# The start of a fused attention and MoE kernel: first loads from two queues, held weights, copies in token order, zeroing on GpSimd

## The chip, the cores and the metric

One core of one Trainium2 chip. The time is device microseconds (us) of the core. Several runs of each kernel are taken, and a comparison uses runs of the same rounds on the same chip. All runs of this study are in the normal state ("fast"). They still differ in one thing, the clock that was granted to TensorE: the profile gives its mean for each run, and it lies between 0.976 and 1.000. The mean leaves something out: in the profiles the records of the clock begin only at 4.26 to 12.35 us, and what lies ahead of them is counted as whole.

Engines: PE is TensorE, PEld its weight loads, DVE is VectorE, ACT ScalarE, POOL GpSimd, SP SyncE. L412 is line 412 of a kernel; the same product has slightly different line numbers in each kernel.

## The reference, cut to what matters

```python
def _attn_ref(q, k, v, f_logit):              # (4, 8, 768, 48) each
    f = 1.0 / (1.0 + np.exp(-f_logit))
    for t in range(S):
        state = f[:, :, t, :, None] * state + einsum('bhd,bhe->bhde', k[:, :, t], v[:, :, t])
        y[:, :, t] = einsum('bhd,bhde->bhe', q[:, :, t], state)

def _moe_ref(x, domain_probs, w1, w2):        # x: (3072, 384), w1: (4, 384, 1024), w2: (4, 1024, 384)
    p = domain_probs / (domain_probs.sum(-1, keepdims=True) + 1e-09)
    for e in range(E):
        h = np.maximum(x @ w1[e], 0.0)
        out += p[:, e:e + 1] * (h @ w2[e])
```

The attention's output is the x of the MoE (mixture of experts).

## The kernel before: the parts that the argument touches

The 768 tokens are worked in six chunks of 128. A planner in the program fixes the order of every engine's instructions ahead of time. In the first chunk, each row of a tile holds two tokens, so that a load moves longer pieces. The loads of that chunk, the pieces of the weights, and their order:

```python
def load(c, nm, b, n):                        # chunk c, tensor nm, batch b
    if (c, nm) == (0, "v"):
        ins[c, nm, b] = nc.gpsimd.dma_start(...)           # v from POOL's queue
        if b in v_gate:
            after(ins[c, nm, b], ins[v_gate[b]])           # v of batch 0 waits for f of batch 1
        return
    if c == 0:
        ins[c, nm, b] = nc.sync.dma_start(...)             # f, k, q of chunk 0 from SP's queue
        return
    ins[c, nm, b] = nc.sync.dma_start(...)
    if (c, nm, b) == (1, "f", 0):
        after(ins[c, nm, b], ins["w", 6])                  # f of chunk 1 waits for the seventh piece of weights
    ...

def load_w(i, e, which, ks, cols):                         # piece i of the weights, from POOL's queue
    ins["w", i] = nc.gpsimd.dma_start(...)
    if i in w_hold:
        after(ins["w", i], ins[w_hold[i]])                 # w_hold = {1: (0, "k", 3)}: held until that load landed

def dma_kc(n):                                             # keys times gates, put back in token order: kc
    k = tl("qk", 0, n)[:, 1].rearrange("(p b) h d -> b p (h d)", b=2)
    for b in range(2):
        nc.sync.dma_start(out=kc[n // 2][...], in_=k[b])

def pe_kv0(g):                                             # new state = kc times v, for two batches
    ...  nc.tensor.matmul(out=tl("KV", 0, 2 * g + b)[...], lhsT=flat(kc[g][tok, i // 2], ...), ...)
# ... cut ...
```

`kc` goes by DMA from SBUF to SBUF, on SP's queue, behind f of chunk 1. Two zeroed buffers (Sf, and Sb twice) are filled by DVE. Q and K of the first chunk are copied out of PSUM in an order that puts even tokens first.

## Time and profile before

| | before |
|---|---|
| time, median of 4 runs | 306.87 us (306.65 to 307.14) |
| span of the profiled run, granted clock | 304.6 us, 0.983 |
| first product of the MoE | 23.40 us |
| kc landed | 46.7 to 49.1 us |
| kc used first | 49.25 us |
| kc used for batches 2 and 3 | 54.34 us |

The prediction below reads most of this profile. First TensorE in order of time, of the kernel before. The columns are start (us), busy time, engine, line, operation, output <- inputs, shape, count; a wait stands at the end in brackets.

```profile
43.97 0.81 PE L479 MATMUL ps_m<-xT,w_sb 128*128 128x512 bf16 x3
...
49.25 0.51 PE L417 MATMUL ps_t<-v,kc 64*128 64x96 bf16 x16
...
54.34 0.51 PE L417 MATMUL ps_t<-v,kc 64*128 64x96 bf16 x16
```

L479 is the first product of the MoE. L417 uses kc. The kc of these batches landed at 46.7 to about 48.1: the slack was about 1.2 us, no more. Then DVE in order of time, of the kernel before:

```profile
3.12 0.17 DVE L168 CAST parb<-par 128x2 bf16<-128x2 f32 x1
3.20 0.42 DVE L171 TENSOR_SCALAR Ui<-U,par 128x64 bf16<-128x64 f32 x2
...
7.71 0.54 DVE L349 TENSOR_TENSOR qk<-k,e 128x384 bf16<-128x384 f32 x1
```

L349 at 7.71 is the first product of keys and gates.

### The profile page before, as it was taken

How to read it: one execution, taken by the hardware profiler on the slowest of the kernel's cores; microseconds unless marked ns; L12 is line 12 of the kernel's file. 1: busy time of each engine (PE TensorE's matmuls, PEld its weight loads, DVE VectorE, ACT ScalarE, POOL GpSimd, SP SyncE). 2: the span in 40 equal slices, each digit the busy share in tenths (PEclk: the TensorE clock that was granted, in tenths of full speed). 3: DMA queues.
4: the chain of work that ended last, by engine and by line, in shares of the span. 5: the costliest groups of instructions: out<-in, count | busy, mean ns of one | idle time of the engine just before them, and what ended most of it. 6: DMA issues, size and time to landing. Idle time of an engine off the chain costs nothing.

```text
span 304.6 us, 5812 instructions
## 1 busy us (share of the span) xinstructions
PE 294.1 (97%) x2265; PEld 176.4 (58%) x2265; DVE 137.4 (45%) x275; ACT 170.7 (56%) x316; POOL 104.4 (34%) x178
## 2 busy tenths in 40 slices
PE   5969999999999999999999999999999999999995
PEld 2636865556776777455556455555555555555553
DVE  8754614697574586216465151534351322201223
ACT  4733554756757466776556765445565544465430
POOL 5192003718378359303628726224320000000000
PEclk9975999999999999999999999999999999999999
DMA  6999999992899987999796943001432100100002
GB/s 171 198 158 187 208 195 222 209 188 59 164 181 199 180 176 145 228 214 192 160 213 107 219 93 48 17 12 34 114 74 50 26 0 26 68 12 2 0 0 104
DMA packets 128975, 36.96 MB, mean 121 GB/s; under 512 B 118812, under 2 KB 128156, under 8 KB 128948
## 3 DMA queue, kind: packets, MB, share of 16 engines
q1 hardware_dynamic: 119748, 29.88, 48.9%
q0 software_dynamic: 9200, 6.72, 15.2%
q8 instruction: 17, 0.28, 0.4%
q14 instruction: 10, 0.08, 0.1%
HBM read 31.51 MB, written 4.72 MB: 119 GB/s over the span
## 4 chain that ended last, share of the span: by engine, by line
PE 87%; DMA 5%; SPq 5%; DVE 2%; ACT 1%; issue 0%; DVEq 0%
PE ps_m L479 39%; PE ps_m L494 39%; DMA q<-in_q_dram 3%; SPq L259 2%; DMA f<-in_f_logit_dram 2%; PE ps_t L425 2%; SPq L261 1%; PE ps_t L445 1%; PE ps_t L441 1%; PE ps_t L311 1%; PE ps_t L451 1%; PE ps_t L362 1%; DVE qk L349 1%; SPq L377 1%; PE ps_t L470 0%
## 5 line engine op out<-in xcount | busy, mean ns | idle before, releaser
L479 PE MATMUL ps_m<-xT,w_sb 128*128 128x512 bf16 (+1 forms) x720 | 155.6, 340 | 0.2 <-DVE pn L296 0.2
L490 ACT ACTIVATE h<-ps_m 128x512 bf16<-128x512 f32 (+1 forms) x188 | 99.6, 532 | 98.4 <-PE ps_m L479 96.1
L494 PE MATMUL ps_m<-w_sb,h 128*128 128x384 bf16 (+1 forms) x776 | 153.5, 324 | 0.0
L494 PEld LDWEIGHTS <-h 128*128 128x128 bf16 x776 | 74.6, 98 | 57.2
L479 PEld LDWEIGHTS <-w_sb 128*128 128x128 bf16 x720 | 68.7, 99 | 42.4 <-issue 0.6
L501 DVE SCALAR_TENSOR_TENSOR o<-ps_m,pn,o 128x384 f32<-128x384 f32 (+1 forms) x73 | 44.7, 612 | 106.2 <-PE ps_m L494 98.8
L488 DVE TENSOR_SCALAR h<-ps_m 128x256 bf16<-128x256 f32 (+1 forms) x52 | 25.0, 490 | 23.6 <-PE ps_m L479 21.1
L465 POOL TENSOR_TENSOR Sf<-Sf,egs 48x192 f32<-48x192 f32 x40 | 20.1, 501 | 43.6 <-DVE Sf L458 41.6
L353 POOL TENSOR_TENSOR qk<-q,e 128x384 bf16<-128x384 f32 x18 | 21.4, 1193 | 25.4 <-ACT e L336 23.1
L336 ACT ACTIVATE e<-ps_t 128x384 f32<-128x384 f32 x48 | 26.5, 667 | 4.3 <-PE ps_t L311 2.3
L434 DVE TENSOR_TENSOR AT<-ps_t,mask 128x512 bf16<-128x512 f32 x40 | 24.9, 683 | 4.8 <-PE ps_t L425 4.8
L247 POOL CAST vb<-v 128x384 bf16<-128x384 f32 x16 | 7.9, 507 | 34.7 <-issue 15.9
L353 POOL TENSOR_TENSOR qk<-k,e 128x384 bf16<-128x384 f32 x18 | 17.9, 998 | 4.5 <-DMA k<-in_k_dram 3.1
L458 DVE TENSOR_TENSOR Sf<-Sf,ps_t 48x192 f32<-48x192 f32 x40 | 14.0, 349 | 10.7 <-PE ps_t L451 8.2
L503 ACT ACTIVATE o<-ps_m,pn 128x384 f32<-128x384 f32 x22 | 12.8, 580 | 4.2 <-PE ps_m L494 3.3
L466 POOL CAST sb<-Sf 48x192 bf16<-48x192 f32 x40 | 14.1, 353 | 2.6
L299 ACT ACTIVATE ex<-f 128x768 f32<-128x768 f32 (+1 forms) x14 | 10.5, 747 | 6.9 <-DMA f<-in_f_logit_dram 6.9
L270 POOL DMA_DIRECT2D w_sb<-in_moe_w_dram x11 | 9.0, 818 | 6.8 <-DMA k<-in_k_dram 6.6
L306 ACT ACTIVATE gp<-ex 128x768 bf16<-128x768 f32 (+1 forms) x14 | 10.5, 751 | 0.4
L811 PE MATMUL ps_m<-busy 128*128 128x512 bf16 x19 | 8.9, 561 | 1.5 <-DVE busy L145 1.5
L445 PE MATMUL ps_t<-vb,AT 128*128 128x48 bf16 x160 | 10.0, 185 | 0.0
L343 POOL DMA_DIRECT2D egs<-e x16 | 9.0, 562 | 2.9 <-ACT e L336 2.9
(81 smaller groups left out, 143.2 us busy)
## 6 DMA issues: line engine op xcount, KB each, us to landing
w_sb<-in_moe_w_dram POOLq DMA_DIRECT2D x5, 768.0 KB, 15.8
k<-in_k_dram SPq DMA_DIRECT2D x10, 384.0 KB, 4.4
q<-in_q_dram SPq DMA_DIRECT2D x10, 384.0 KB, 5.5
v<-in_v_dram SPq DMA_DIRECT2D x10, 384.0 KB, 5.7
out_dram<-o SPq DMA_DIRECT2D x19, 192.0 KB, 2.1
f<-in_f_logit_dram SPq DMA_DIRECT2D x9, 384.0 KB, 5.1
w_sb<-in_moe_w_dram POOLq DMA_DIRECT2D x6, 384.0 KB, 7.3
f<-in_f_logit_dram SPq DMA_DIRECT2D x6, 192.0 KB, 4.2
```

What stands on the lines that cost most here:

```text
L336: nc.scalar.activation(out=o, in_=i, func=AF.Exp, scale=1.0 if j else -1.0)
L353: engines[eng].tensor_tensor(out=tl("qk", c, b)[:, j, :, 0:D].rearrange("t (i r) d -> t i r d", r=2), in0=tl("qk"[j], c, b // 2)[:, hh(b), ...
L434: nc.vector.tensor_tensor(out=tl("AT", c, b)[:, r].rearrange("s i t -> s (i t)"), in0=tl("A", c, b, r).rearrange("s i t -> s (i t)"), in1= ...
L445: nc.tensor.matmul(out=y[:, h * D:(h + 1) * D], lhsT=AT[:, r, i, :], rhs=vb[:, h, :], start=(c == 0), stop=True, skip_group_check=True)
L458: nc.vector.tensor_tensor(out=Sf[rows, b], in0=Sf[rows, b], in1=KV[rows, :, r, :], op=ALU.add)
L465: nc.gpsimd.tensor_tensor(out=Sf[rows, b], in0=Sf[rows, b], in1=eg, op=ALU.mult)
L466: nc.gpsimd.tensor_copy(out=nb[rows, b, :, r * D:(r + 1) * D], in_=Sf[rows, b])
L479: nc.tensor.matmul(out=hp(c, e, fc, n0, n1, nf)[:, f], lhsT=w1_sb[:, e, kk, (fc + f) * 128:(fc + f + 1) * 128], rhs=tl("xT", c)[:, kk, n0: ...
L488: nc.vector.tensor_relu(out=dst, in_=src)
L490: nc.scalar.activation(out=dst, in_=src, func=AF.Relu)
L494: nc.tensor.matmul(out=tl("op", c, e, nt, part)[:, cols], lhsT=tl("h", c, e, half_of(c, nt * T))[:, fc, nt * T:(nt + 1) * T], rhs=w2_sb[:, ...
L501: nc.vector.scalar_tensor_tensor(out=o, in0=op, scalar=pe, in1=o, op0=ALU.mult, op1=ALU.add)
```

## The change

It tries to bring the start of the MoE forward. The first loads come from two queues at once; the pieces of weights wait until loads of the later batches are through; the zeroing leaves DVE; the copies of Q and K become plain, and the matmul reads with a stride instead. The planner's costs are adjusted, which reorders TensorE's program.

```diff
-    nc.scalar.preload_act_table_set("natural_log_exp_and_others")
...
-    nc.vector.memset(Sf, 0.0)
+    nc.gpsimd.memset(Sf, 0.0)
...
-        nc.vector.memset(t, 0.0)
+        nc.gpsimd.memset(t, 0.0)
...
-            ins[c, nm, b] = nc.sync.dma_start(out=t[b % 2], in_=srcs[nm, 0][b])
+            ins[c, nm, b] = (nc.scalar if b == 1 else nc.sync).dma_start(out=t[b % 2], in_=srcs[nm, 0][b])
...
-        if c == 0:
-            o, i = o.rearrange("m q i (b p) -> m (q i) b p", b=2), i.rearrange("m q i (p b) -> m (q i) b p", b=2)
         copy(eng, o, i)
...
-        Q = QK[:, 0].rearrange("m (j i) t -> m i j t", i=2)
+        Q = QK[:, 0].rearrange("m (j i) (p b) -> m i b j p", i=2, b=2)
...
-                                         lhsT=QK[rows, 1, 2 * j + i, tok], rhs=Q[rows, i, :, tok], start=True, stop=True)
+                                         lhsT=QK[rows, 1, 2 * j + i, b::2], rhs=Q[rows, i, b], start=True, stop=True)
...
-    v_gate, w_hold, issued = {0: (0, "f", 1)}, {1: (0, "k", 3)}, []
+    v_gate, w_hold, issued = {0: (0, "f", 1)}, {0: (0, "k", 2), 1: (0, "q", 2)}, []
...
+        elif b == 1:
+            iss = P.add(f"issue {nm}", {"ACT": 0.65}, lambda _, nm=nm: load(0, nm, 1, 1), ...)
+            ...
+            if nm == "f":
+                P.add("table", {"ACT": 1.3}, lambda _: nc.scalar.preload_act_table_set("natural_log_exp_and_others"), ...)
... (planner costs and lags: cut)
```

More of the change, by code (lines that the diff above doesn't have):

```diff
@@ L45, in ready @@
                 return None
-            t = max(t, d.end + (d.lag + self.LATENCY if d.engine != e else 0.0 if e == "PE" else 0.05))
+            t = max(t, d.end + (d.lag + self.LATENCY if d.engine != e else 0.0 if e == "PE" or o.name.startswith("gate2 0.") else 0.05))
         return t
@@ L67, in run @@
         free_at = {e: 0.0 for o in left for e in o.costs}
-        free_at.update({"DMA": 0.8, "DVE": 5.0, "POOL": 3.5, "ACT": 2.1, "PE": 2.0})
+        free_at.update({"DMA": 0.8, "DVE": 5.4, "POOL": 4.6, "ACT": 0.7, "PE": 2.0})
         freeing, done, now = [], [], 0.0
@@ L517, in add_load @@
     def add_load(c, nm, b, n, prio, deps=(), cost=None):
-        op = P.add(f"ld {nm}{c}.{b}", {"DMA": cost or (1.05 if c else 0.65) * n}, lambda e: load(c, nm, b, n), prio,
-                   deps=deps, takes=[(nm, c, b // 2)], lag=2.0 if c else 1.65)
+        op = P.add(f"ld {nm}{c}.{b}", {"DMA": cost or (1.05 if c else 0.7) * n}, lambda e: load(c, nm, b, n), prio,
+                   deps=deps, takes=[(nm, c, b // 2)], lag=2.0 if c else 1.6 if b < 2 else 2.3)
         for i in range(n):
@@ L529, in add_v @@
                             deps=issued[-1:] + ([ld[v_gate[b]]] if b in v_gate else []), lag=1.2))
-        ld[0, "v", b] = P.add(f"ld v0.{b}", {"DMA": 0.65}, lambda _: None, prio, deps=issued[-1:], lag=1.6)
+        ld[0, "v", b] = P.add(f"ld v0.{b}", {"DMA": 0.75}, lambda _: None, prio, deps=issued[-1:], lag=1.3)
     for i, x in enumerate("f0 f1 k0 k1 q0 q1 v0 v1 f2 f3 k2 k3 q2 q3".split()):
@@ L535 @@
             add_v(b, -1000 + i)
+        elif b == 1:
+            iss = P.add(f"issue {nm}", {"ACT": 0.65}, lambda _, nm=nm: load(0, nm, 1, 1), -1100 + i, takes=[(nm, 0, 0)], lag=-0.2)
+            ld[0, nm, 1] = P.add(f"ld {nm}0.1", {"DMA": 0.7}, lambda _: None, -1000 + i, deps=[iss], lag=1.6)
+            if nm == "f":
+                P.add("table", {"ACT": 1.3}, lambda _: nc.scalar.preload_act_table_set("natural_log_exp_and_others"), -1100 + i + 0.5)
         else:
@@ L579, in attention0 @@
             pt_ = lambda kind, *x: ("ps_t", kind, 0, n) + x
-            g2 = P.add(f"gates 0.{n}", {"ACT": 0.95}, lambda _, n=n: [gate1(0, n, 1), gate2(0, n, 1)], s(0) - 0.5,
-                       deps=[ld[0, "f", 2 * g], ld[0, "f", 2 * g + 1]], takes=[("ex", 0, n), ("gp", 0, g)], frees=[("f", 0, g), ("ex", 0, n)])
-            cs = P.add(f"cs 0.{n}", {"PE": 0.5}, on(pe_cs, 0, n), s(0), deps=[g2], takes=[pt_("cs")], lag=0.2, frees=[("gp", 0, g)])
+            g1 = P.add(f"gate1 0.{n}", {"ACT": 0.53}, on(gate1, 0, n, 1), s(0) - 0.5, deps=[ld[0, "f", 2 * g], ld[0, "f", 2 * g + 1]],
+                       takes=[("ex", 0, n)], frees=[("f", 0, g)])
+            g2 = P.add(f"gate2 0.{n}", {"ACT": 0.53}, on(gate2, 0, n, 1), s(0) - 0.6, deps=[g1], takes=[("gp", 0, g)], frees=[("ex", 0, n)])
+            cs = P.add(f"cs 0.{n}", {"PE": 0.6}, on(pe_cs, 0, n), s(0), deps=[g2], takes=[pt_("cs")], lag=0.05, frees=[("gp", 0, g)])
             ek = P.add(f"expk 0.{n}", {"ACT": 0.41}, on(exps, 0, n, (1,)), s(0) + 0.1, deps=[cs], takes=[("e", 0, n)], frees=[pt_("cs")])
             eq = P.add(f"expq 0.{n}", {"ACT": 0.55}, on(exps, 0, n, (0,)), s(0) + 0.2, deps=[cs], takes=[("e", 0, n)], frees=[pt_("cs")])
-            pe = {"DVE": 0.5} if n < 2 else {"DVE": 0.5, "POOL": 1.2}
+            pe = {"DVE": 0.55} if n < 2 else {"DVE": 0.55, "POOL": 1.2}
             km = P.add(f"k 0.{n}", pe, one(product, 0, n, 1), s(4) - 0.2, deps=[ek, ld[0, "k", 2 * g], ld[0, "k", 2 * g + 1]],
@@ L590, in attention0 @@
             kcd[n] = P.add(f"kc 0.{n}", {"DMA": 0.4}, on(dma_kc, n), -453 + n, deps=[km, wd[2, 1][0]], frees=[("qk", 0, n)], lag=2.0)
-            tk = P.add(f"tpk 0.{n}", {"PE": 0.22}, on(pe_tp, 0, n, 1), s(4), deps=[km], takes=[pt_("tp")], frees=[("qk", 0, n)], lag=0.2)
-            tq = P.add(f"tpq 0.{n}", {"PE": 0.22}, on(pe_tp, 0, n, 0), s(4) + 0.01, deps=[qm], takes=[pt_("tp")], frees=[("qk", 0, n)], lag=0.2)
-            et = [P.add(f"ev_tp{j} 0.{n}", {"DVE": 0.36, "ACT": 0.5}, one(ev_tp, 0, n, slice(j, j + 1)), s(4) + 0.1, deps=[tj],
+            tk = P.add(f"tpk 0.{n}", {"PE": 0.4}, on(pe_tp, 0, n, 1), s(4), deps=[km], takes=[pt_("tp")], frees=[("qk", 0, n)], lag=0.05)
+            tq = P.add(f"tpq 0.{n}", {"PE": 0.4}, on(pe_tp, 0, n, 0), s(4) + 0.01, deps=[qm], takes=[pt_("tp")], frees=[("qk", 0, n)], lag=0.05)
+            et = [P.add(f"ev_tp{j} 0.{n}", {"DVE": 0.37, "ACT": 0.55}, one(ev_tp, 0, n, slice(j, j + 1)), s(4) + 0.1, deps=[tj],
                         takes=[("QK", 0, n)], frees=[pt_("tp")]) for j, tj in ((1, tk), (0, tq))]
-            at = P.add(f"at 0.{n}", {"PE": 0.5}, on(pe_at0, n), s(7), deps=et, takes=[a_key(n, r) for r in range(2)], lag=0.2, frees=[("QK", 0, n)])
+            at = P.add(f"at 0.{n}", {"PE": 0.5}, on(pe_at0, n), s(7), deps=et, takes=[a_key(n, r) for r in range(2)], lag=0.05, frees=[("QK", 0, n)])
             eA = [P.add(f"ev_at{r} 0.{n}", {"DVE": 0.62}, on(ev_at, 0, n, r), s(7) + 0.1 + 0.1 * r, deps=[at],
@@ L599, in attention0 @@
             N.append(P.add(f"y 0.{n}", {"PE": 0.5}, on(pe_y0, n), s(11), deps=eA + [ld[0, "v", 2 * g], ld[0, "v", 2 * g + 1]] + N[-1:] * (n % 2),
-                           takes=ys, frees=[("AT", 0, n)], lag=0.2))
+                           takes=ys, frees=[("AT", 0, n)], lag=0.05))
             for b in range(2 * g, 2 * g + 2) if n % 2 else ():
@@ L605, in attention0 @@
                 xk = ("ps_t", "xp", 0, b, 0)
-                xt = P.add(f"xt 0.{b}", {"PE": 0.17}, on(pe_xt, 0, b, slice(0, KD)), s(13) + 0.01 * b, deps=[ey], takes=[xk], frees=[("yb", 0, b)], lag=0.2)
+                xt = P.add(f"xt 0.{b}", {"PE": 0.17}, on(pe_xt, 0, b, slice(0, KD)), s(13) + 0.01 * b, deps=[ey], takes=[xk], frees=[("yb", 0, b)], lag=0.05)
                 xdone[0, b] = [P.add(f"ev_xt 0.{b}", {"ACT": 0.45, "DVE": 0.4},
@@ L613, in attention0 @@
             kv = P.add(f"kv 0.{g}", {"PE": 0.36}, on(pe_kv0, g), s15, deps=[kcd[2 * g], kcd[2 * g + 1], xdone[0, B - 1][0]],
-                       takes=[("ps_t", "KV", 0, b) for b in bs], lag=0.2)
+                       takes=[("ps_t", "KV", 0, b) for b in bs], lag=0.05)
             for b in bs:
@@ L747 @@
     pl = P.add("ld p", {"DMA": 0.2}, lambda e: load_p(), -989.5, lag=3.0)
-    pj = P.add("p by j", {"POOL": 0.8, "DVE": 0.6}, lambda e: p_by_j(e), -1.5, deps=[pl] + xdone[0, 1], takes=[("v", 0, 0)])
+    pj = P.add("p by j", {"POOL": 0.8, "DVE": 0.6}, lambda e: p_by_j(e), -1.5, deps=[pl] + xdone[0, B - 1], takes=[("v", 0, 0)])
     pp = P.add("pp", {"PE": 0.6}, lambda e: pe_pp(), -1, deps=[pj], takes=[("ps_m", "pp")], lag=0.2, frees=[("v", 0, 0)])
```

## The prediction

> **What bounds the kernel now.** I read the page first, then the chain of work that ended last, then the order of time on TensorE around the start of the MoE (mixture of experts: L479 is its first product, L494 its second), then busy time by stretch, then who waited for whom.
>
> The page:
>
> ```profile
> PE 294.1 (97%) x2265; PEld 176.4 (58%) x2265; DVE 137.4 (45%) x275; ACT 170.7 (56%) x316; POOL 104.4 (34%) x178
> ...
> PEclk9975999999999999999999999999999999999999
> DMA  6999999992899987999796943001432100100002
> ```
>
> TensorE is busy 97% of 304.6 us, and the waits of PE from 22 us to the end are two of 0.2 us. So the MoE stage runs at TensorE's pace, and this change removes none of its matmuls: it can only start it earlier, or run its beginning at a better clock. The third and fourth slice (15 to 30 us) have a low clock, and the DMA engines are busy nearly to 68 us.
>
> The chain of waits, first 30 us:
>
> ```profile
> 9.18 8.75 DMA q<-in_q_dram
> ...
> 18.05 1.84 DVE qk L349 x2
> ...
> 19.94 1.03 PE ps_t L362 x8
> ```
>
> The last load of the first 128 tokens (q of batch 3) lands at 17.9; its products and transposes follow. TensorE in order of time:
>
> ```profile
> 17.49 0.40 PE L362 MATMUL ps_t<-ident,qk 128*128 128x128 bf16 x4 [2.27 <-POOL qk L349]
> ...
> 19.94 1.03 PE L362 MATMUL ps_t<-ident,qk 128*128 128x128 bf16 x8 [0.66 <-DVE qk L349]
> 20.77 0.85 PE L470 MATMUL ps_t<-ident,yb 128*128 128x128 bf16 x6
> ...
> 23.40 0.82 PE L479 MATMUL ps_m<-xT,w_sb 128*128 128x256 bf16 x3
> ```
>
> TensorE takes instructions in program order. The transposes of batches 2 and 3 (L362, waiting for late loads) stand ahead of the transposes L470 of the finished batches 0 and 1. So the MoE starts at 23.40, though the first two batches were through their masking on DVE at 16.0.
>
> By stretch (us, PE, PEld, DVE, ACT, POOL busy, granted clock, DMA share, GB/s):
>
> ```profile
> 12.35:19.17 6.82, 4.44 (x95) 2.77 (x93) 4.20 (x7) 3.60 (x11) 3.49 (x4) 1.00 1.17 180
> ...
> 23.40:29.41 6.01, 6.01 (x62) 3.90 (x58) 2.38 (x5) 1.92 (x5) 1.70 (x3) 0.50 1.25 187
> 29.41:36.50 7.09, 6.87 (x74) 6.00 (x69) 5.42 (x15) 4.55 (x12) 0.00 (x0) 1.00 1.21 207
> ```
>
> The first 6.0 us of the MoE run at clock 0.50, so about 3.0 us are lost there: at full clock the same work would have started at 26.4.
>
> **What the Trainium skill says.** "TensorE: Matmul & The Clock Gate", part 1: the clock is halved after a window of some 3.4 us with little activity and given back after a busy one. The trace agrees in kind: PE stood still 2.27 us before 17.49, and the clock is 0.50 from 19.2 to 29.4, three such windows. "DMA: Bandwidth & Descriptors", "Issuing engines are not separate DMA queues": a second issuing engine saves only the sequencer's time. Before, one issue takes 0.64 us on SP and the first six loads land 0.8 us apart (3.8 to 7.9), so there is little to save. "VectorE: DVE Perf Modes", "Zero memsets can be issued as uint32": the trace has the two bf16 zeroings on DVE as 112x768 uint32, 0.70 each; the program of the changed kernel has them on POOL as 112x1536, twice the elements.
>
> **The change part by part.**
>
> 1. Loads of batch 1 from ACT. f of batch 1 is issued at 0.74 with f of batch 0 instead of 1.58; k and q of batch 1 come after the 1.28 us table load, at about 2.7 and 3.3. The first gate began at 5.11, when f of batch 1 had landed (4.7) and was seen; now about 4.3. Saves 0.8 on this chain.
>
> 2. Zeroing on POOL. DVE was in memsets to 7.68 (0.70 + 1.51) and began the first product at 7.71. Now it is free at 5.5, so the product starts when exp of k is ready, about 6.9. POOL pays: three fills of 128 f32 take 0.49, some 1.0 to 1.1 ns per element, so 768 + 2 x 1536 elements take 3.9 (estimate). POOL is free near 6.4, and v of batch 0 is issued at 6.4 instead of 5.32. It is needed by L409, at 14.67 before and about 12.2 after: close, but with fewer loads ahead of it.
>
> 3. Copies in token order. The eight copies of Q and K of 512 columns cost 0.69 on DVE and 0.58 on ACT; the new order sends the first four to ACT, so the four products run on DVE without a break (6.9 to 9.1; the fourth ended at 11.65). Then copies to 10.8 (from ACT's 8.5, 4 x 0.58), first masking at 10.7, 4 x 0.64, ended 13.3 instead of 16.0: 2.7 saved. The stride-2 reads move to L394 on PE, 16 matmuls in 0.42; even doubled that is 0.4 per batch.
>
> 4. Weights held. The first weight piece (issued at 6.87, landed 14.4) shared the engines with k and q of batches 2 and 3. A piece alone takes 2.0 us (landings 26.6, 28.5, 30.5). It now waits for k of batch 2, so q of batch 3 lands near 13 instead of 17.9 (12 loads at 0.75, two v at 0.8, from 2.2 us, plus latency).
>
> 5. Order on TensorE. The program now puts the last product of attention and the transposes L470 of batches 0 and 1 ahead of the transposes of batch 3, and moves the transposes of the probabilities (1.3 us at half clock) later. Working on: yb copied at about 15.6, batch 2's transposes and copies 15 to 16.2, scores 16.9, first L479 near **17.5** instead of 23.4. PE is thinly used from 10 to 17 us, so I expect half clock again for 6 to 8 us of the MoE: 3 to 4 us lost, against 3.0 before. The lead in full-clock terms is then 26.4 - 21 = about **5 us**.
>
> 6. What is behind: the transfers. Weight pieces 2 to 4 landed at 20.8, 23.3, 26.6, because they were issued at 15.6, 17.4, 19.4 behind waits. Now they can be issued from about 13 in one go. If the DMA engines work without a break from 2.2: 12 loads 9.4, four v 3.3, p 0.2, four pieces 8.0, and then the 21.9 us from 26.6 to 48.4 as before: all pieces but the last landed at 45.0 instead of 48.4. So the stream gains **3.4 us**. In it stands a stage with no slack: the reordered keys kc, issued after the sixth piece of weights and landing together:
>
> ```profile
> SPq L261 <- DMA w_sb<-in_moe_w_dram: 24.3, 1, 24.3
> ...
> SPq L374 <- DMA f<-in_f_logit_dram: 6.4, 1, 6.4
> ```
>
> The first kc for batches 0 and 1 were issued at 35.05 to 37.4 and landed 11.3 to 11.6 later, 46.7 to about 48; TensorE used them (L417) at 49.25. In the new program L417 stands one unit of seven matmuls (1.3 us) earlier. TensorE with a lead of 5 would come there at 43; kc would be there at about 44.6. Then the lead is the stream's: 3.4, or a bit less. After that, slack is larger (f of the next tokens landed 50.0, used 54.9), the last weight piece (67.0, needed 68.5) moves with both, and the load of f at 84.56 (0.2 us waited for) hangs on work that moves with TensorE.
>
> The sum: 306.7 - 3.5 = **303.2**.
>
> **The rivals.** (a) TensorE sets the gain alone: the stream advances as far as the head, or kc has more slack; then 5 us, 301.7, and with a full clock from the start 8, 298.5. For it: the steady state has no waits; against it: kc had 1.2 us of slack at most. (b) The stream gains little: holding the weights leaves the DMA engines idle while POOL, in program order, waits for the issue (DMA share fell to 0.77 at 16 to 18 us from such a wait). Then the MoE starts early and waits for its second to fourth piece, and a stop of 2 to 3 us halves the clock again: 305 to 306. For it: POOL now waits for two loads, not one, with v of batches 2 and 3 behind the first. (c) Zeroing on POOL delays v of batches 0 and 1, L409 waits, the head gains 3 instead of 6: about 304.5, as the stream still sets the later part. (d) A new wait at the next tokens' loads gives all back: 306.5; little speaks for it.
>
> **Range and chances.** The two limits are 5 +- 2 (clock) and 3.4 +- 1 (stream), the smaller counts. Range 300.4 to 305.6. Over 2% needs 300.7 or less, which wants (a) with a good clock: 0.14. Slower by 2% has no mechanism of that size: 0.02.
>
> **What would show it.** First L479 at 17 to 18.5 (right), at 20 or later (steps 3 to 5 wrong). First gate near 4.3; masking ended near 13.3; q of batch 3 landed near 13; pieces of weights landed without gaps, the ninth at about 45. Clock 0.5 in the first 6 us of the MoE. A wait of PE of 1 to 2 us before L417, or before a weight load near 19 to 23 us. The forecast is wrong upward if the clock is whole from the first L479 and kc lands before 42; wrong downward if PE waits over 2 us in several places from 18 to 50.

## The result, and the profile after

| | before | after |
|---|---|---|
| time, median of 4 runs | 306.87 us (306.65 to 307.14) | 303.46 us (301.41 to 304.13) |
| ratio after / before | | 0.9877, 95% 0.9828 to 0.9926 |
| span and clock of the profiled run | 304.6 us, 0.983 | 301.4 us, 0.994 |

A ratio here is the mean time of one kernel's fast runs over that of the other's of the same rounds, so it is not quite the ratio of the medians. The kernel is 1.2% faster, within 2% and inside the predicted range. A second set of five runs, later, gave 302.15 (below).

From the page of the changed kernel (busy time by engine, then the clock and the DMA engines in 40 slices of 7.5 us, then the chain by engine):

```profile
PE 290.9 (97%) x2261; PEld 173.2 (57%) x2261; DVE 133.9 (44%) x265; ACT 172.5 (57%) x323; POOL 107.5 (36%) x181
...
PEclk9999997999999999999999999999999999999999
DMA  7999999964979979999699952101432100100002
...
PE 83%; DMA 10%; SPq 3%; DVE 1%; POOL 1%; ACT 1%; issue 0%
```

The low clock has gone from the third and fourth slice, and a new low stands in the seventh (45 to 53 us). The chain of work that ended last now holds DMA for 10% of the span. TensorE in order of time, of the changed kernel:

```profile
16.94 0.83 PE L476 MATMUL ps_m<-xT,w_sb 128*128 128x256 bf16 x6
...
42.93 0.21 PE L414 MATMUL ps_t<-v,kc 64*128 64x96 bf16 x1 [1.12 <-DMA kc<-qk]
43.52 0.34 PE L414 MATMUL ps_t<-v,kc 64*128 64x96 bf16 x7 [0.38 <-DMA kc<-qk]
...
44.55 0.34 PE L414 MATMUL ps_t<-v,kc 64*128 64x96 bf16 x7 [0.31 <-DMA kc<-qk]
...
46.40 1.49 PE L476 MATMUL ps_m<-xT,w_sb 128*128 128x512 bf16 x3
...
51.80 0.51 PE L414 MATMUL ps_t<-v,kc 64*128 64x96 bf16 x16
```

The MoE starts at 16.94 instead of 23.40, and its first 512-column product at 36.46 instead of 43.97: at that point the lead is 7.5 us. Then TensorE stands before L414, where kc is used. The 16 matmuls that ran in one go in the kernel before now trickle from 42.93 to 44.89, as the transfers land. At 46.40 the same products take 1.49 instead of 0.81: half clock. Who waited for whom, PE from 18 us to the end, total, times, longest:

```profile
PE ps_t L414 <- DMA kc<-qk: 2.0, 4, 1.1
```

And by stretch (PE, PEld, DVE, ACT, POOL busy, granted clock, DMA share, GB/s):

```profile
36.50:45.84 9.34, 7.37 (x51) 3.71 (x50) 2.05 (x5) 3.13 (x6) 0.44 (x1) 1.00 1.12 204
45.84:49.25 3.41, 3.41 (x11) 1.43 (x10) 0.59 (x2) 1.03 (x2) 2.92 (x8) 0.50 1.20 229
```

PE is busy 7.37 of 9.34 us in the first stretch, and the next 3.41 us run at clock 0.50, which costs half of it, 1.7 us. The account of the profiled runs therefore closes: the last product with kc ended 49.77 before and 44.89 after, 4.9 earlier; minus 1.7 for the half clock is 3.2, and the spans differ by 304.6 - 301.4 = 3.2.

### The profile page after: what moved, and what is told of

It is laid out like the page before. It is cut to its first block, busy times and chain, and to the rows that moved or that the text cites. A ratio compares the mean times of both kernels' runs of the same rounds, so it can differ in the third digit from the quotient of the medians.

```text
span 301.4 us, 5811 instructions
## 1 busy us (share of the span) xinstructions
PE 290.9 (97%) x2261; PEld 173.2 (57%) x2261; DVE 133.9 (44%) x265; ACT 172.5 (57%) x323; POOL 107.5 (36%) x181
## 3 DMA queue, kind: packets, MB, share of 16 engines
q1 hardware_dynamic: 118164, 29.29, 48.4%
## 4 chain that ended last, share of the span: by engine, by line
PE 83%; DMA 10%; SPq 3%; DVE 1%; POOL 1%; ACT 1%; issue 0%
PE ps_m L491 38%; PE ps_m L476 38%; DMA kc<-qk 4%; DMA w_sb<-in_moe_w_dram 3%; DMA f<-in_f_logit_dram 2%; PE ps_t L422 2%; DMA k<-in_k_dram 2%; SPq L260 2%; PE ps_t L442 1%; SPq L258 1%; PE ps_t L438 1%; PE ps_t L310 1%; PE ps_t L448 1%; POOL w_sb L269 0%; POOL v L252 0%; SPq L374 0%
## 5 line engine op out<-in xcount | busy, mean ns | idle before, releaser
L487 ACT ACTIVATE h<-ps_m 128x512 bf16<-128x512 f32 (+1 forms) x188 | 98.4, 527 | 98.2 <-PE ps_m L476 96.0
L498 DVE SCALAR_TENSOR_TENSOR o<-ps_m,pn,o 128x384 f32<-128x384 f32 (+1 forms) x73 | 44.6, 611 | 108.6 <-PE ps_m L491 100.7
L476 PEld LDWEIGHTS <-w_sb 128*128 128x128 bf16 x720 | 68.0, 98 | 42.6 <-issue 1.5
L485 DVE TENSOR_SCALAR h<-ps_m 128x256 bf16<-128x256 f32 (+1 forms) x52 | 26.1, 510 | 22.8 <-PE ps_m L476 20.2
L246 POOL CAST vb<-v 128x384 bf16<-128x384 f32 x17 | 8.7, 523 | 32.1 <-issue 14.7
L455 DVE TENSOR_TENSOR Sf<-Sf,ps_t 48x192 f32<-48x192 f32 x40 | 14.0, 351 | 13.2 <-PE ps_t L448 9.6
L244 ACT CAST yb<-ps_t 128x384 bf16<-128x384 f32 x17 | 8.1, 476 | 6.2 <-PE ps_t L442 6.2
```

What stands on the lines that cost most here:

```text
L455: nc.vector.tensor_tensor(out=Sf[rows, b], in0=Sf[rows, b], in1=KV[rows, :, r, :], op=ALU.add)
L476: nc.tensor.matmul(out=hp(c, e, fc, n0, n1, nf)[:, f], lhsT=w1_sb[:, e, kk, (fc + f) * 128:(fc + f + 1) * 128], rhs=tl("xT", c)[:, kk, n0: ...
L485: nc.vector.tensor_relu(out=dst, in_=src)
L487: nc.scalar.activation(out=dst, in_=src, func=AF.Relu)
L498: nc.vector.scalar_tensor_tensor(out=o, in0=op, scalar=pe, in1=o, op0=ALU.mult, op1=ALU.add)
```

## The experiments

Twelve kernels ran in three sets, each set on one chip beside the kernel before (medians 306.29, 307.64 and 306.04, 9 to 11 runs). First the whole picture. The columns come from each trace: the start of the MoE, the landing of the first and last kc transfer, the first and last use of kc for batches 0 and 1, and the start of its use for batches 2 and 3 (second use).

| kernel | median us | ratio to before | MoE starts | kc landed | kc first use | second use | span | span minus second use |
|---|---|---|---|---|---|---|---|---|
| before | 306.87 | 1 | 23.40 | 46.7 to 49.1 | 49.25 to 49.77 | 54.34 | 304.6 | 250.3 |
| changed | 303.46 | 0.9877 | 16.94 | 42.9 to 45.6 | 42.93 to 44.89 | 51.80 | 301.4 | 249.6 |
| changed, again | 302.15 | 0.9863 | 17.72 | 43.1 to 45.5 | 43.12 to 45.09 | 50.32 | 299.7 | 249.4 |
| kc ahead of f | 299.04 | 0.9764 | 17.51 | 36.4 to 41.6 | 41.72 to 42.23 | 47.46 | 297.3 | 249.8 |
| fillers in the stop | 301.66 | 0.9850 | 17.71 | 43.0 to 45.1 | 44.51 to 45.02 | 50.25 | 300.1 | 249.8 |
| one queue only | 305.97 | 0.9983 | 18.41 | 45.3 to 47.6 | 45.39 to 47.22 | 53.74 | 303.4 | 249.7 |
| weights not held | 301.14 | 0.9823 | 18.20 | 42.1 to 44.4 | 42.41 to 43.91 | 49.13 | 299.1 | 250.0 |
| not held, kc first | 301.55 | 0.9842 | 19.98 | 35.8 to 40.8 | 44.19 to 44.70 | 49.93 | 299.4 | 249.5 |
| before, kc first | 304.92 | 0.9948 | 23.83 | 40.3 to 45.9 | 47.54 to 48.06 | 52.63 | 302.8 | 250.2 |
| before, two queues | 304.22 | 0.9932 | 21.59 | 45.4 to 47.8 | 45.41 to 47.32 | 51.90 | 301.7 | 249.8 |

The last column says where to look: from the second use of kc on, all these kernels need 249.4 to 250.3 us (the four of the last experiments, which are not in the table, 249.3 to 250.5). What this change gains or loses in these profiles is decided in the first 54 us.

My theory: two things can hold TensorE at about 42 to 48 us, the start of the MoE (the "head") and the landing of kc (the "stream"), and the later one counts. The rivals: the head alone sets the gain; or what matters is the clock, and the wait for kc is only where it shows.

### kc ahead of f (label e1_kcfirst)

The transfers of kc are issued on SP before f of chunk 1 instead of behind it; TensorE's order is kept.

```diff
     def load(c, nm, b, n, now=False):
+        if (c, nm, b) == (1, "f", 0) and not now:
+            return
...
     def dma_kc(n):
-            nc.sync.dma_start(out=kc[...], in_=k[b])
+            d = nc.sync.dma_start(out=kc[...], in_=k[b])
+            if (n, b) == (0, 0):
+                after(d, ins["w", 6])
+        if n == B - 1:
+            load(1, "f", 0, 1, True)
```

> The changed kernel with the eight transfers of reordered keys (kc) issued ahead of the first load of f of the next tokens, after the same (seventh) piece of weights; the order on every compute engine is unchanged. Theory (the gain is capped by kc, and the wait for it also costs a stretch of half clock): kc lands by 36, TensorE does not stop before L414 (2.9 us before), the clock stays whole from 4.9 us on, span 301.4 - 2.9 - 1.7 = 296.8, time near 298.7 (over 2.5% faster than the kernel before). Rival (the next loads give it back: f then lands later and TensorE stops at the next tokens' cumulative sums, L310, instead): time 301 to 303.

Measured: 299.04 us (298.73 to 299.16), ratio 0.9764 (0.9739 to 0.9788), clock 0.998 or more in every run. TensorE in order of time:

```profile
41.72 0.51 PE L420 MATMUL ps_t<-v,kc 64*128 64x96 bf16 x16
...
47.46 0.51 PE L420 MATMUL ps_t<-v,kc 64*128 64x96 bf16 x16
```

The 16 matmuls run in one go again, at 41.72. From issue to landing, the transfers of kc took (minimum, median, maximum), first in the changed kernel, then here:

```profile
DMA to landing us min/median/max: 3.2/10.5/11.5
```

```profile
DMA to landing us min/median/max: 5.3/6.0/6.7
```

In the changed kernel those of batches 0 and 1 took 10.9 to 11.5, issued behind f; the 3.2 is the last of the eight, issued only when f had landed. Here those of batches 0 and 1 landed at 36.4 to 39.5, a little later than the 36 expected, but in time. The stop and the half clock are both gone, and the rival's new stop did not come (TensorE waited 0.7 us at its cumulative sums, 0.6 in the changed kernel), so the theory holds: the changed kernel had been giving back 1.1% of the time, over 3 us (ratio 0.9764 against 0.9877), at this one place.

### Fillers in the stop (label e2_warm)

Twelve matmuls that nobody needs stand ahead of the first use of kc, so that TensorE has work while it would wait.

```diff
     def pe_kv0(g):
+        for _ in range(12 if g == 0 else 0):
+            nc.tensor.matmul(out=tl("KV", 0, 0), lhsT=busy[:, 0:128], rhs=busy, start=True, stop=True)
```

> The changed kernel with 12 matmuls of ones (128x512, 0.22 us each) on TensorE just ahead of the first L414, so that it is busy while it waits for kc. Theory (waiting and half clock are two costs, the second follows from the first): L414 still ends its wait at about 44.6, but the clock stays whole, 1.7 us less: span 299.7, time near 301.6. Rival (the clock drop at 45.8 has nothing to do with the stop): the drop remains, time 303.5 or a little more.

Measured: 301.66 us (301.25 to 302.13), ratio 0.9850 (0.9824 to 0.9875), clock 0.998 to 1.000. TensorE in order of time:

```profile
41.82 2.75 PE L411 MATMUL ps_t<-busy 128*128 128x512 bf16 x12
44.51 0.51 PE L416 MATMUL ps_t<-v,kc 64*128 64x96 bf16 x16
```

The fillers take the place of the wait, and the use of kc ends at 45.02, as late as without them (44.89, and 45.09 in the second profile below). The stop costs the same; the half clock behind it is taken away, in all five runs. So the clock is a second cost that follows from the stop, and the rival "it is the clock" is wrong for the larger part: with a whole clock in both, 301.66 - 299.04 = 2.6 us on the same chip are the stop, but for 0.2 us by which the MoE started later here.

### The changed kernel again (label e12_after)

> The changed kernel itself once more, on the chip of this call, so that the others can be read against it and so that chips can be told from kernels. Expected 302.5 to 303.9, ratio 0.985 to 0.991, a stop of 2 to 3 us before the key-value products and one window of half clock behind it. If the first submission was a chance of its chip, the ratio is outside that.

Measured: 302.15 us (301.44 to 303.67), ratio 0.9863 (0.9815 to 0.9911). TensorE in order of time:

```profile
43.12 0.21 PE L414 MATMUL ps_t<-v,kc 64*128 64x96 bf16 x1 [1.13 <-DMA kc<-qk]
43.70 0.70 PE L414 MATMUL ps_t<-v,kc 64*128 64x96 bf16 x8 [0.36 <-DMA kc<-qk]
...
50.32 0.52 PE L414 MATMUL ps_t<-v,kc 64*128 64x96 bf16 x16
```

The stop is the same, but in this profile no half clock followed, and the second use is at 50.32 instead of 51.80. The time is a little under the expected 302.5 to 303.9, and the expected window of half clock did not come in this profile. That is instructive. The nine runs of the changed kernel in both sets fall in two groups: clock 0.999 or 1.000, 301.41, 301.44, 301.45 and 302.15 us; clock 0.993 or 0.994, 303.18, 303.19, 303.67, 303.74 and 304.13. Their means are 1.97 us apart, near the 1.7 that one window of half clock costs. One window of 3.41 us at half clock in 301 us gives just that mean, 1 - 1.7 / 301 = 0.994. The stop is in both profiles; the half clock is in one, and by the clocks in five of the nine runs (where in those runs it fell is seen only in the profiled one).

The traces show part of the reason. Within a profile the changes of the clock lie multiples of 3.41 us apart (19.17 and 29.41 in the kernel before, 45.84 and 49.25 in the changed one), so the time can be cut into steps of 3.41 us from them. In the first profile one step (42.42 to 45.84) held most of the stop: PE was busy for 2.06 us of it. Here the stop fell across two steps, with 2.60 and 2.24 us busy. Of the other profiles with over 1 us of waits for kc, e3_zlate (1.04 busy in the emptiest step) and e5_sp (1.49) had a half clock behind the stop; e4_zdve (2.01) and e7_perm (2.54) had none. The emptiest steps had it, but 2.01 without and 2.06 with half clock show that the busy time alone does not decide it.

The clock at the start differs too, and the mean does not show it. In this profile the records begin at 12.10:

```profile
8.03 1.01 PE L814 MATMUL ps_m<-busy 128*128 128x512 bf16 x2
...
12.74 0.60 PE L814 MATMUL ps_m<-busy 128*128 128x512 bf16 x2
```

In the first profile such a pair took 0.59 already at 7.26. That profile had a favourable start: its MoE began at 16.94, here at 17.72.

### One queue only (label e5_sp)

```diff
-            ins[c, nm, b] = (nc.scalar if b == 1 else nc.sync).dma_start(out=t[b % 2], in_=srcs[nm, 0][b])
+            ins[c, nm, b] = nc.sync.dma_start(out=t[b % 2], in_=srcs[nm, 0][b])
```

> The changed kernel with the loads of batch 1 issued from SP again (one part undone). Theory: f of batch 1 lands at 4.7 instead of 3.9 and the first gate starts at 5.1, but the first cumulative sum moves by 0.3 us only, as it waited for VectorE; SP is busy for three more issues of 0.65 us, so k of batch 2 lands 1 us later, and with it weights and kc: time 303.9 to 304.6. Rival (transfers set the pace, a second issuing engine is worth nothing): 303.5.

Measured: 305.97 us (305.21 to 307.52), ratio 0.9983 (0.9923 to 1.0043). The loss is larger than I expected: without the second queue nearly the whole gain is gone. A part of it is the clock, as no run of this kernel was free of a half clock (0.989 or 0.993). Among the runs at 0.992 to 0.994 this kernel took 305.21 to 305.97 us, the changed kernel 303.18 to 304.13, and the kernel before, on the chip of this kernel, 305.55 and 305.62. So at like clock the queue is worth about 2.0 us, or 0.7%, and that is still nearly the whole gain. What that queue does is seen by stretch, from 2.75 to 8.25 us. First the kernel with one queue:

```profile
2.75:5.50 2.75, 1.45 (x4) 0.26 (x2) 2.72 (x6) 0.51 (x1) 2.75 (x3) 1.00 1.02 258
5.50:8.25 2.75, 2.13 (x18) 1.65 (x19) 2.56 (x11) 2.45 (x8) 1.89 (x3) 1.00 0.99 250
```

Then the changed kernel, with two:

```profile
2.75:5.50 2.75, 1.45 (x4) 0.27 (x2) 2.72 (x6) 0.91 (x3) 2.75 (x3) 1.00 1.13 308
5.50:8.25 2.75, 1.86 (x19) 1.09 (x20) 2.60 (x12) 2.55 (x8) 1.88 (x3) 1.00 1.18 326
```

The last column is what the DMA engines moved: 258 and 250 GB/s with SP's queue alone for f, k and q, 308 and 326 with two (POOL's queue, for v, is there in both). SP issues one load of 192 KB every 0.68 us in this trace, which is at most 289 GB/s (196,608 bytes over 0.68 us). One queue fed the engines more slowly than they could move. Their busy share, the column ahead, is 1.02 and 0.99 with one queue, and so would pass for engines at their limit.

q of batches 2 and 3 is issued from 7.33 us on with two queues and from 8.85 with one, and q of batch 3 lands at 12.39 instead of 14.05; the first piece of weights, held for k of batch 2, is issued at 9.87 instead of 12.02; kc lands 2.0 to 2.4 us earlier.

### The kernel before with the second queue alone (label e11_act_alone)

f, k and q of batch 1 are issued from ACT's queue, with the table load between f and k; nothing else.

```diff
-    nc.scalar.preload_act_table_set("natural_log_exp_and_others")
...
-            t = tl(nm, c, b // 2)[:].rearrange(...)
-            ins[c, nm, b] = nc.sync.dma_start(out=t[b % 2], in_=srcs[nm, 0][b])
+            for x in "fkq" if (nm, b) == ("f", 1) else nm if b != 1 else "":
+                t = tl(x, c, b // 2)[:].rearrange(...)
+                ins[c, x, b] = (nc.scalar if b == 1 else nc.sync).dma_start(out=t[b % 2], in_=srcs[x, 0][b])
+                if (x, b) == ("f", 1):
+                    nc.scalar.preload_act_table_set("natural_log_exp_and_others")
```

> The kernel before with one part of the change alone: f, k and q of batch 1 issued from ACT's queue (table load after f). Theory (the second issuing queue takes three issues of 0.65 us off SP, so that the loads of batches 2 and 3 start nearly 2 us earlier; q of batch 3 lands near 16.3 instead of 17.9, the first product of the MoE is at 21.8 instead of 23.4, and the weights behind it are earlier by as much): 304.8 to 305.6, ratio 0.994 to 0.997. Rival (the prediction's first step: little to save in the issuing): 306.2 to 306.8, ratio above 0.998.

Measured: 304.22 us (303.49 to 306.32), ratio 0.9932 (0.9882 to 0.9981), a little better than expected; the rival (above 0.998) lies at the very edge of the interval. At like clock (0.992 to 0.994) this kernel took 303.49 to 304.36 us and the kernel before, on the same chip, 305.49 to 306.04, so the rival is out. The MoE starts at 21.59 (expected 21.8), q of batch 3 lands at 16.31 (expected 16.3). TensorE in order of time, one of the uses of kc:

```profile
45.96 0.34 PE L419 MATMUL ps_t<-v,kc 64*128 64x96 bf16 x7 [0.33 <-DMA kc<-qk]
```

This one part, alone, brings 1 - 0.9932 = 0.7% of the 1.4% that the changed kernel brings in the same set, and already here TensorE arrives at kc before it has landed (0.8 us of waits): in this profile the stream is the limit from there on.

### Weights not held (label e6_unhold)

The changed kernel with the holds of the kernel before: the first piece free, the second behind k of batch 3.

```diff
-        if i in w_hold:
+        if i == 1:
+            after(ins["w", i], ins[0, "k", 3])
+        elif i in w_hold and i > 1:
             after(ins["w", i], ins[w_hold[i]])
```

> The changed kernel with the first piece of weights not held and the second held by k of batch 3, as before (one part undone). Theory: the first piece lands near 13, q of batch 3 near 15 instead of 12.4, first L476 at 18 to 19 instead of 16.9; the seventh piece of weights and kc land at most 1 us later, because the engines move the same bytes without a break: TensorE stops for kc for less time, total 303.3 to 304.5. Rival (the head counts): as much as L476 is late, 304.5 to 305.5.

Measured: 301.14 us (300.88 to 302.63), ratio 0.9823 (0.9771 to 0.9875). I expected a small loss against the changed kernel, and it came out no slower, if anything 0.4 to 0.5% faster (the intervals overlap; among the runs with a whole clock it took 300.88 to 301.14 us, the changed kernel 301.41 to 302.15). The head was later, 18.20 instead of 16.94, as expected. But the first piece of weights was issued at 7.36 instead of 9.87, the seventh landed at 29.79 instead of 30.89, and kc with it:

```profile
42.41 0.58 PE L416 MATMUL ps_t<-v,kc 64*128 64x96 bf16 x8
43.29 0.62 PE L416 MATMUL ps_t<-v,kc 64*128 64x96 bf16 x8 [0.30 <-DMA kc<-qk]
```

Waits of 0.30 and 0.06 are left of the 2.0. Holding the weights is good for the head (both profiles had a whole clock from 4.9 us or earlier), and in the changed kernel a later head costs nothing. That holding is bad for the stream is not shown: with the holds the seventh piece landed at 30.89 and 30.42 in the two profiles of the changed kernel and at 30.19 to 31.10 in e1_kcfirst, e2_warm and e7_perm, and in the second profile without holds (next) at 30.44.

### Weights not held, kc ahead of f (label e10_kc_unhold)

Two edits: one was faster alone, the other no slower.

> The changed kernel with both of the edits that were faster alone: kc ahead of f, and the first weights not held for the late loads. Theory A (with the stop at the key-value products gone, TensorE is bound by the start of the MoE alone; not holding costs 1.2 us there, 18.2 against 16.9 to 17.5, and the earlier stream is worth nothing more): 299.3 to 300.2, not faster than kc ahead of f alone (299.0). Theory B (the stream still sets a part): 297.5 to 298.6. Both: no wait for kc, whole clock from before the first product of the MoE.

Measured: 301.55 us (301.20 to 302.10), ratio 0.9842 (0.9785 to 0.9898). Neither forecast was met: it is slower than kc ahead of f with the holds kept (299.04, ratio 0.9764), by more than theory A put. With kc out of the way the head counts, and the head suffers. Who waited for whom on PE from 16 us, then TensorE in order of time:

```profile
PE ps_t L365 <- DVE qk L352: 1.5, 1, 1.5
```

```profile
16.69 0.61 PE L365 MATMUL ps_t<-ident,qk 128*128 128x128 bf16 x4 [1.55 <-DVE qk L352]
...
19.98 0.83 PE L484 MATMUL ps_m<-xT,w_sb 128*128 128x256 bf16 x6
```

The transposes of batch 2 wait 1.55 us for their products, as they did in the kernel before, and a window of half clock (16.17 to 19.58) falls on the last steps ahead of the MoE: it starts at 19.98. That is 2.5 us later than with the holds, and the second use of kc is 2.5 later too (49.93 and 47.46). So the same edit costs nothing, or gains some 0.5%, where the stream is the limit, and loses about 0.8% where the head is. Not all of the 2.5 us need be the edit: in the profile above, with the same first loads and no holds, the clock was whole from 4.75 on and the MoE started at 18.20. Here it was whole from 9.34 on, as with kc ahead of f (9.37), but then fell, which it did not there. Three of the four runs had a clock of 0.994; the one at 1.000 took 301.28, so the loss does not hang on that window alone. (The two kernels with kc first ran on different chips; their ratios are each to the kernel before on the same chip.)

### The kernel before with kc ahead of f (label e9_bkc)

> Control: the kernel before, with kc issued ahead of f of the next tokens and right after the seventh piece of weights, the same edit that brought the changed kernel to 299.0. Theory (kc ahead of f only takes away TensorE's stop before the key-value products, which the kernel before doesn't have: its kc landed by 48 and was used at 49.25): the same as the kernel before within 0.5 us, ratio 0.998 to 1.002, first product of the MoE at 23.4, key-value products at 49.2. Rival (the order of kc and f is worth something by itself, apart from the stop): 303 to 305, ratio below 0.995.

Measured: 304.92 us (304.57 to 305.86), ratio 0.9948 (0.9905 to 0.9992). My forecast of no effect is missed by about 1 us, and the rival's numbers fit. I had reckoned with the one profile of the kernel before, in which kc had 1.2 us of slack and a half clock over the first 6 us of the MoE. In this profile the half clock fell at 12.55 to 22.79, ahead of the MoE at 23.83, and kc was used at 47.54, 1.7 earlier than in that profile, when the kernel before would not have had all of it.

```profile
47.54 0.52 PE L423 MATMUL ps_t<-v,kc 64*128 64x96 bf16 x16
```

A floor fits that: the profiled run of the kernel before took 306.4, and minus 1.2 of slack is 305.2; of its 29 runs in the three sets the lowest is 305.16, although their clock goes up to 0.994. No second profile of the kernel before was taken in a run of better clock, so this reading is argued, not shown. By the ratios the edit is worth 0.5% here and 1.1% in the changed kernel: more there, as the theory has it, but not nothing here, as I had put it.

### Zeroing, and the order of the copies (labels e3_zlate, e4_zdve, e8_best, e7_perm)

In the first, the fills on GpSimd are moved behind the weights; in the second they go back to DVE:

```diff
-    nc.gpsimd.memset(Sf, 0.0)          # and both of Sb; e3: issued in load_w, at i == 9
+    nc.vector.memset(Sf, 0.0)          # e4
```

> The changed kernel with the zeroing of Sf and Sb on GpSimd moved behind the issue of the weights. Theory on the start (the fills on GpSimd held a cast and two tensor_scalar of VectorE for 2.7 us each): these three take 0.2 us each again, first cumulative sum L314 at about 5.7 instead of 5.99, first product at about 7.0 instead of 7.65, first L476 0.3 to 0.7 earlier. The total does not move by more than 0.5 us if kc sets it: 303.0 to 303.8. Rival (the head sets the total): 0.5 us or more faster.

> The changed kernel with the zeroing of Sf and Sb put back on VectorE (one part undone; the order on all other engines unchanged). The prediction's step 2 would have it that VectorE's first product slips by 0.8 us or more. Theory now: it does not, since on GpSimd the fills held VectorE for 2.7 us anyway: first product at 7.7 (7.65 in the changed kernel). GpSimd is free at 2.5 and issues v at 4.2 instead of 5.8, so v goes ahead of k of batch 2, the first weights are issued near 11.3 instead of 9.9 as in the run with late zeroing, and kc lands 1 to 2 us later: time 304 to 305. If v's order did not matter: 303.5.

Measured: 303.38 us (301.67 to 305.99), ratio 0.9912 (0.9867 to 0.9958), and 304.07 us (301.68 to 306.08), ratio 0.9903 (0.9839 to 0.9967). Neither is told apart from the changed kernel by its time. In the trace there is a clear effect. DVE and then POOL in order of time, of the changed kernel:

```profile
3.13 2.73 DVE L167 CAST parb<-par 128x2 bf16<-128x2 f32 x1
3.20 2.73 DVE L170 TENSOR_SCALAR Ui<-U,par 128x64 bf16<-128x64 f32 x2
...
7.65 0.54 DVE L348 TENSOR_TENSOR qk<-k,e 128x384 bf16<-128x384 f32 x1
```

```profile
3.13 2.70 POOL L186 MEMSET sb<- 112x1536 bf16 x2
```

and DVE with the fills moved away:

```profile
3.13 0.17 DVE L167 CAST parb<-par 128x2 bf16<-128x2 f32 x1
3.21 0.42 DVE L170 TENSOR_SCALAR Ui<-U,par 128x64 bf16<-128x64 f32 x2
...
7.10 0.56 DVE L349 TENSOR_TENSOR qk<-k,e 128x384 bf16<-128x384 f32 x1 [1.67 <-ACT e L336]
```

A cast of two columns took 2.73 us, exactly while GpSimd filled. The next two edits show that the fills were the cause: with the fills behind the weights or back on DVE the cast took 0.17 again. This fits what the Trainium skill, "SBUF — State Buffer", "Who interferes with whom", says: a DVE cast or tensor_scalar can need the port pair that it shares with GpSimd, and whoever holds it first blocks the other; that it was the ports is not shown by these runs. So moving the fills freed DVE of 2.2 us and cost it 2.3 there, and the first product starts at 7.65 instead of 7.71. With the fills moved away it starts at 7.10. But the gain did not reach the MoE, which started at 17.89: v was then issued at about 4.2, ahead of k of batch 2, the weights held for that k were issued at 11.35 instead of 9.87, and the wait for kc grew to 2.9 us. With the fills back on DVE the first product started at 7.71 (7.7 was expected) and v was issued at 4.07. The median of 304.07 is as forecast, but the reason is not seen in the profile (of the run of 301.68): the first weights were issued at 10.53, not 11.3, and the waits for kc were 2.0 us, as in the changed kernel.

kc ahead of f, with the fills moved behind the weights as well:

> Both edits at once: kc issued ahead of f, zeroing behind the weights. Theory: with kc out of the way the head counts again, but the second to fourth piece of weights had only waits of 0.35 us, so at most some 0.3 us more than kc alone: time 298.4 to 298.7. Rival (the head counts in full): 298.0.

Measured: 299.77 us (298.56 to 301.13), ratio 0.9782 (0.9747 to 0.9817); the MoE started at 18.49. No better than kc ahead of f alone, and neither forecast was met. Three runs took 298.56 to 299.01 and three 300.53 to 301.13, all with a mean clock of 0.999 or 1.000, so what is counted as half clock does not explain this scatter.

Last, the copies of Q and K in the order of the kernel before, within the changed kernel:

```diff
     def ev_tp(c, b, js, eng):
+        if c == 0:
+            o, i = o.rearrange("m q i (b p) -> m (q i) b p", b=2), i.rearrange("m q i (p b) -> m (q i) b p", b=2)
         copy(eng, o, i)
... (and the two reads in pe_at0 as before)
```

> The changed kernel with Q and K copied in the split order again, the scores read without a stride (one part undone). Theory: the copies on VectorE take 0.69 instead of 0.42 us, those on ACT stay at 0.58, L391 unchanged at 0.43 for 16; first L476 later by 0.3 us or less, and the total unchanged since kc sets it: 303.2 to 303.8. Rival: the strided reads cost more than the copies save, then faster than 303.2.

Measured: 302.45 us (302.08 to 303.89), ratio 0.9858 (0.9807 to 0.9910), the same as the changed kernel by these ratios. The time is under the 303.2 to 303.8 that was forecast, in the range of the rival, but so was the changed kernel's own second set (302.15). The MoE started at 17.98, 0.3 us after the later of the changed kernel's two profiles (16.94 and 17.72); masking began at 11.52 instead of 10.74. The waits for kc were 1.1 us instead of 2.0: the later head took up part of the stop.

## Why the prediction was right, and where it was not

- **That the stream of transfers limits the gain (step 6): right.** The change moved the stream by 3.6 us (ninth of the eleven pieces of weights: 38.98 against 42.61; tenth, which is the one that the prediction put at 45.0 instead of 48.4: 44.83), kc landed from 42.9 to 45.6 (predicted 44.6), and TensorE waited for it 2.0 us. kc ahead of f shows by test that this was the limit.
- **That the gain equals the stream's, 3.4: wrong, by two terms that cancel, so that 303.2 against 303.46 is in part luck.** The kernel before had 1.2 us of slack at kc, which the changed kernel used up too: the last use ended 4.9 earlier, 3.6 + 1.2 (the rest is rounding of where a landing is seen). And a window of half clock behind the stop took 1.7 back in the profiled run. 4.9 - 1.7 = 3.2. In runs without that window the gain is the whole 4.9: 306.4 - 4.9 = 301.5, and those runs took 301.41 to 302.15. Rival (a) had put a full clock and no limit by the stream at 298.5; with kc out of the way the kernel took 299.04.
- **The clock (step 5): wrong place.** Half clock for 6 to 8 us was predicted at the start of the MoE; the clock was whole there (from 4.88 on). Hence the lead of TensorE before the stop was 7.5 us, not 5. It did not matter, as the stream was the limit, except that the stop became longer.
- **The first queue (step 1): the step that failed most.** "So there is little to save" (in the part on the Trainium skill) was read from landings 0.8 us apart, and took the DMA engines for the limit. The queue was: 250 GB/s from one, 326 from two. Taking this part back costs nearly all of the gain (ratio 0.9983), and doing it alone brings half (0.9932). So the 3.4 of the stream (3.6 measured) was right for a reason that was not the main one: steps 4 and 6 credited it to the order and the holds of the weights, but the tenth piece landed at 44.83 in the changed kernel, 46.85 with one queue and 43.70 without the holds (48.44 before). What step 1 did count, the first gate, began at 4.58 (4.3 predicted, 5.11 before). The k and q of batch 1 were also issued at 1.51 and 2.17, not 2.7 and 3.3, while ACT was loading its table (1.48 to 2.76): the queue did not wait for the table.
- **The zeroing (step 2): a wrong gain.** First product 7.65 and not 6.9. GpSimd's fills held DVE for 2.7 us, and the fills took 0.74 + 2.70 us, somewhat under the 3.9 estimated (0.49 us for three fills of 128 is 1.3 ns per element, not 1.0 to 1.1, and the fills themselves took 0.9).
- **Copies (step 3), holds (step 4), order (step 5):** masking ended at 13.2 (predicted 13.3), q of batch 3 landed at 12.39 (near 13), the MoE started at 16.94 (17.5). The numbers are right. But the holds, counted as a gain, brought no time in the changed kernel, since the stream and not the head was the limit: without them it took 301.14, if anything less.
- **Rival (b)**, waits for the second to fourth piece of weights, came only as two waits of 0.35 us; **rival (d)** didn't come.

Still open: what part of the scatter between runs of a kernel comes from where the half clock falls, in the kernel before; why moving the fills makes single runs as long as 305.99; and what the new order on TensorE is worth, which no run undid. Nor was the other way out of the stop tried, to put the use of kc later in TensorE's order. A part of the scatter lies outside the span: the time is mostly 1.8 us longer than the span, but 3.4 in one run (303.89 and 300.5, e7_perm).

## What to carry to other kernels

When an engine's start is brought forward, list every transfer that it meets later, with its slack, and move those that are small and needed early ahead of large ones that are needed late: here one reordering of kc and f, without any new work, was worth nearly as much again as the whole change (1.1% on top of 1.2%; 299.04 us). A busy share of 1.0 of the DMA engines does not say that they are the limit; compare the GB/s of stretches, and the issue interval times the size of a load. Two edits that are each harmless or a gain alone need not add up: each moves a limit, and which limit counts decides what it is worth.

## What the Trainium skill lacked or had wrong

- "DMA: Bandwidth & Descriptors", "Issuing engines are not separate DMA queues", says that a second issuing engine saves only sequencer time, usually small. Here, with loads of 192 KB issued 0.68 us apart, it raised the rate from 250 to 258 up to 308 to 326 GB/s in the first 8 us, and its removal cost about 2.0 us at like clock, 0.7% of the whole time. It is sequencer time that was saved, three issues of 0.62 to 0.72 us on ACT's queue; but it was not small.
- "TensorE: Matmul & The Clock Gate", part 1, puts the half clock after an idle window of some 3.4 us, but does not say how little work makes a window idle. Here waits of 2.0 us in all, with single matmuls between them, were enough in one of two profiles of the changed kernel (in five of nine runs, by the clock). A window with PE busy for 2.06 of 3.41 us was followed by half clock, one with 2.01 (e4_zdve) was not. The cost, when it came, was one window of 3.41 us at 0.50.
- No page that I used says how long a small transfer takes when it is issued behind large ones: kc of batches 0 and 1 took 10.9 to 11.5 us behind f and the weights, and 5.3 to 6.7 us ahead of f (64 KB each; f 192 KB).
